# The last wo's fourth rows by four transfers of eight partitions, and the unread products ahead of the last values

## The chip, the cores and the metric

The kernel runs on one core of a Trainium2 chip. The metric is the device time of one execution in microseconds; the median of the runs is compared. A profiled execution of the same program gives the views that are quoted.

## The reference

A decode step for 8 sequences: a grouped-query attention over a cache of 8192 positions and, on the same normalised input, a dense layer with Mish and a second dense layer. Both results and the input are added up.

```python
xn = _layernorm(x)                                   # x: 8 x 1 x 512
q = (xn @ wq).reshape(B, Sq, 32, 128)                # 32 heads, 8 of keys and values
scores = einsum("bhqd,bhkd->bhqk", q, k) * 128**-0.5 # k, v: 8 x 8 x 8192 x 128
o = einsum("bhqk,bhkd->bhqd", softmax(scores), v)
a = o.reshape(B, Sq, 4096) @ wo                      # wo: 4096 x 512
h = xn @ w1 + b1                                     # w1: 512 x 1792
m = (h * tanh(softplus(h))) @ w2                     # w2: 1792 x 512
return x + a + m
```

All is float32. The caches are 537 MB of the 561 MB that are read.

## The kernel before

The work goes in 16 packs (`PACKS`) of two batch entries (`PB`) and two key heads; four pairs of key heads (`PAIRS`) with four packs each. For each pack and batch entry (b = 0, 1) one block of keys and one block of values is loaded, 8 MB each. `scores` multiplies the keys, `rows`, `maximum`, `exponents`, `fold` and `weights` make the softmax weights on ACT and DVE, `values` multiplies the weights with the values of the pack before, `gather` and `merge` turn the result into columns `oT`. After four packs `turn` transposes the pair's `oT` into `oW`, and `outputs` multiplies it with the pair's part of `wo`. One TensorE instruction of float32 shows as two matmul records and two weight loads.

All loads are issued by the SP queue, in the order of a list (`queue`). There are three places in SBUF: `kva`, `kvb` (20 rows of 1024 numbers on each partition) and `kvw` (four rows). A load is taken from the head of the list (`pump`) once its place is free by the program's order, and the DMA instruction then waits for those matmuls that still read the columns that it overwrites. The DMA completions are told by eight semaphores, handed out in turn.

At the end the list holds the values of the last pack, for b = 0 into `kvb` and for b = 1 into `kva` in two parts (three quarters and one), and then six pieces: `w2` in four parts (`W2_PARTS`: two, two, two and one of seven rows), into `kvb`, and between them the last pair's `wo` in two halves, into `kvw`. Each partition's part of a pair's `wo` is four rows of 1024 numbers (`OR = 4`); a half is two rows of all 128 partitions.

The program's last steps, in the order in which PE gets them:

```python
values(0, landed["v", p, 0]); gather(p, 0); sums(p, lsel.pop(p)); merge(p, 0); add_up()
values(1, landed["v", p, 1], 0, ROUNDS * 3 // 4)
values(1, landed["v", p, 1], ROUNDS * 3 // 4); gather(p, 1)
down(*W2_PARTS[0], w2_sb)
keep_busy(2)
merge(p, 1); turn(PAIRS - 1, tid)
down(*W2_PARTS[1], w2_sb); last_outputs(0, OR // 2, wo_sb)
down(*W2_PARTS[2], w2_sb); last_outputs(OR // 2, OR, wo_sb)
down(*W2_PARTS[3], w2_sb)
```

`down` (L628) multiplies the Mish result with parts of `w2`, 16 matmuls for two rows of it; `last_outputs` (L562) the last pair's `oW` with rows of `wo`, 8 matmuls for a row: two heads, four groups of 128 output columns. Both add into the same PSUM tile `H`, as `add_up` (L548) does, which starts it. `turn` (L514) writes `oW` from PSUM by four copies of 32 partitions each, two on DVE (L528) and two on ACT (L526), which follow one upon the other. `keep_busy(n)` (L639) makes n matmuls of 512 columns into a PSUM tile that nobody reads afterwards; they only keep TensorE at work. After the last `down` DVE copies `H` (L718) and SP stores it (L719).

Of the kernel before, what the change touches and what calls it, by code (L numbers as in the profile page):

```python
# [8 lines left out]
F32 = mybir.dt.float32  # L9
# [4 lines left out]
P = 128  # L14
B = 8
# [8 lines left out]
G = 4  # L24
# [3 lines left out]
BW = 1024  # L28
# [4 lines left out]
Q = P // G  # L33
# [5 lines left out]
PAIRS = HKV // 2  # L39
NP = B // PB  # L40
PACKS = PAIRS * NP
R = P // G
# [22 lines left out]
QR = CC  # L65
OR = 4
W1R = 2 * CC * P // P
W2R = G * FT // 2 * FP // P
FAR = 1e38

# [2 lines left out]
def kernel(  # L73
# [12 lines left out]
    nc = tc.nc  # L86
# [3 lines left out]
    work = ctx.enter_context(tc.tile_pool(name="work", bufs=2))  # L90
# [4 lines left out]
    place = {n: const.tile([P, size], F32, name=f"kv{n}") for n, size in sizes.items()}  # L95
    queue = []
    taken, landed = {}, {}

    def rows_of(blocks):

        return blocks.rearrange("j p f -> (j p f)").rearrange("(p f) -> p f", p=P)
# [12 lines left out]
    def plan(what, at, blocks, parts=((0, 1),), lo=0):  # L114

        rows = rows_of(blocks)
        n = rows.shape[1]
        t = place[at][:, lo : lo + n]

        def load(cols):  # L120
            nc.sync.dma_start(t[:, cols], rows[:, cols])
            return t

        for first, end in parts:
            cols = slice(round(first * n), round(end * n))
            queue.append((what, at, lambda cols=cols: load(cols)))


    sc = const.tile([P, 512], F32, name="sc")
# [7 lines left out]
    def blocks_of(src, p, b):  # L137
        i, k = divmod(p, NP)
        lo = ((k * PB + b) * HKV + 2 * i) * NB
        return src[lo : lo + KN]  # L140
# [3 lines left out]
    def plan_k(p, b):  # L144
        if (p, b) == (0, 1):
            plan(("k", p, b), "a", blocks_of(kT, p, b))
        else:
            up[0] = KX * BW - up[0]
            plan(("k", p, b), "b", blocks_of(kT, p, b), lo=up[0])

    def plan_v(p, b, at, parts=((0, 1),)):
        plan(("v", p, b), at, blocks_of(v, p, b), parts)

# [3 lines left out]
    def plan_wo(i, parts=((0, 1),)):  # L157
        plan(("wo", i), "w", wo[i * 4 : i * 4 + 4], parts)
# [8 lines left out]
    for p in range(PACKS):  # L167
        for b in range(PB):
            plan_k(p, b)
            if (p, b) in between:  # L170
                what, i = between[p, b]
                (plan_wq if what == "wq" else plan_wo)(i)
            if p > 0:
                plan_v(p - 1, b, "a")
    plan_v(PACKS - 1, 0, "b")
    plan_v(PACKS - 1, 1, "a", ((0, 3 / 4), (3 / 4, 1)))
    W2_PARTS = ((0, 2), (2, 4), (4, 6), (6, 7))
    for k, (lo, hi) in enumerate(W2_PARTS):
        plan("w2", "b", w2, ((lo / W2R, hi / W2R),))
        if 0 < k < 3:  # L180
            plan_wo(PAIRS - 1, (((k - 1) / 2, k / 2),))


    S = psum.tile([P, GK], F32, name="s")
# [34 lines left out]
    xnT = const.tile([P, QR, 2, Q], F32, name="xnT")  # L219
    aT = const.tile([P, 2 * W2R, Q], F32, name="aT")  # L220
    xw = aT.rearrange("p j q -> p (j q)")[:, : W1R * 2 * B]
    xw = xw.rearrange("p (r t b) -> p r t b", r=W1R, t=2)

    def setup():
# [33 lines left out]

        wide = scratch[:B, 2 * D : 2 * D + W1R * P]
        for t in range(2):  # L260
            nc.gpsimd.tensor_copy(
                wide.rearrange("b (r c t i) -> b r c t i", r=W1R, c=CC, t=2)[:, :, :, t, :],
                xc.rearrange("b (c i r) -> b r c i", c=CC, r=W1R),
            )
# [26 lines left out]
    def setup_w1(wide):  # L291
        for r in range(W1R):
            nc.tensor.transpose(
                M[:, 64 + r * B : 64 + (r + 1) * B], wide[:, r * P : (r + 1) * P], ident[:B, :B]
            )
        for t in range(2):
            nc.vector.tensor_scalar(
                xw[:, :, t, :],
                M[:, 64 : 64 + W1R * B].rearrange("p (r b) -> p r b", r=W1R),
                half[:, t : t + 1],  # L300
                None,
                op0=ALU.mult,
            )

        nc.gpsimd.memset(pt, 0.0)
# [148 lines left out]
    def values(b, vt, lo=0, hi=ROUNDS):  # L454


        for k in range(lo, hi):
            for c in range(G):
                j = G * k + c
                nc.tensor.matmul(  # L460
                    O[b][Q * c : Q * (c + 1), :],
                    pt[:, b, j % 2, j // 2].rearrange("p t e h -> p (t e h)"),
                    vt[:, W4 * DH * j : W4 * DH * (j + 1)],
                    start=(k == 0),
                    stop=(k == ROUNDS - 1),
                )

    def gather(p, b):

        os = OS[p, b] = work.tile([P, DH], F32, name="os")  # L470
        nc.vector.tensor_scalar(os, O[b][:, :DH], isel[:, 0:1], None, op0=ALU.mult)  # L471
        for i in range(1, W4):
            nc.vector.scalar_tensor_tensor(  # L473
                os,
                O[b][:, DH * i : DH * (i + 1)],
                isel[:, i : i + 1],
                os,
                op0=ALU.mult,
                op1=ALU.add,
            )  # L480

    oT, oW = {}, {}

    def merge(p, b):

        i, k = divmod(p, NP)
        at = 168 + b * 2 * REP
        nc.tensor.matmul(M[:, at : at + 2 * REP], OS.pop((p, b)), hsel, start=True, stop=True)  # L488
        if b == PB - 1:
            if k == 0:  # L490
                oT[i] = work.tile([P, 2, REP, B], F32, name="oT")
            nc.vector.tensor_mul(  # L492
                oT[i][:, :, :, k * PB : (k + 1) * PB].rearrange("p e h b -> p (e h) b"),
                M[:, 168 : 168 + PB * 2 * REP].rearrange("p (b r) -> p r b", b=PB),
                RT.pop(p).rearrange("p b e h -> p (e h) b"),
            )
# [10 lines left out]
    def turn(i, tid):  # L507


        to = oW[i] = work.tile([P, OR, 2, B], F32, name="oW")  # L510
        o = oT.pop(i).rearrange("p n h b -> p (n h b)")
        cols = 2 * REP * B
        for r in range(OR):
            nc.tensor.matmul(  # L514
                M[:, 256 + r * cols : 256 + (r + 1) * cols],
                tid[:, r].rearrange("p g i -> p (g i)"),
                o,
                start=True,
                stop=True,
            )  # L520
        m = M[:, 256 : 256 + OR * cols].rearrange("p (r j q) -> p j r q", r=OR, j=G)
        for j in range(G):
            rows = slice(Q * j, Q * (j + 1))
            dst = to[rows].rearrange("p r h b -> p r (h b)")
            if i == PAIRS - 1 and j % 2:
                nc.scalar.copy(dst, m[rows, j])  # L526
            else:
                nc.vector.tensor_copy(dst, m[rows, j])  # L528

    def outputs(i, w):  # L530

# [13 lines left out]
    def add_up():  # L545

        for g in range(G):
            nc.tensor.matmul(  # L548
                H[Q * g : Q * g + B, :P],
                rsel[:, :B],  # L550
                acc[:, g * P : (g + 1) * P],
                start=True,
                stop=False,
            )

    def last_outputs(lo, hi, w):

        for r in range(lo, hi):
            for h in range(2):
                for g in range(G):  # L560
                    at = r * BW + h * D + g * P
                    nc.tensor.matmul(  # L562
                        H[Q * g : Q * g + B, :P],
                        oW[PAIRS - 1][:, r, h, :],
                        w[:, at : at + P],
                        start=False,
                        stop=False,
                    )

    def mish(w1_sb):  # L570
# [42 lines left out]
        for e in range(2):  # L613
            nc.vector.tensor_mul(
                act.rearrange("p (i a e l) -> p e a l i", a=2, e=2, i=W2R)[:, e],
                h[:, half * e : half * (e + 1)].rearrange("p (a l i) -> p a l i", a=2, i=W2R),
                t1[:, half * e : half * (e + 1)].rearrange("p (a l i) -> p a l i", a=2, i=W2R),
            )
# [4 lines left out]
    def down(lo, hi, w):  # L623

        for j in range(2 * lo, 2 * hi):
            for g in range(G):
# [5 lines left out]
                    start=False,  # L632
                    stop=(j == 2 * W2R - 1),
                )

    def keep_busy(n):

        for k in range(n):
            nc.tensor.matmul(C[0][:Q, :], ones[:, :Q], acc, start=True, stop=True)  # L639
# [19 lines left out]
    for p in range(PACKS):  # L659
        for b in range(PB):  # L660
            k = landed.pop(("k", p, b))

            n = PB * p + b - (p > 0)
# [15 lines left out]
            if (p, b) in between:  # L679
                what, i = between[p, b]  # L680
# [14 lines left out]
    p = PACKS - 1  # L695
# [5 lines left out]
    sums(p, lsel.pop(p))  # L701
    merge(p, 0)
    add_up()
    values(1, landed["v", p, 1], 0, ROUNDS * 3 // 4)
    values(1, landed["v", p, 1], ROUNDS * 3 // 4)
    gather(p, 1)
    w2_sb, wo_sb = landed["w2"], landed["wo", PAIRS - 1]
    down(*W2_PARTS[0], w2_sb)
    keep_busy(2)
    merge(p, 1)  # L710
    turn(PAIRS - 1, tid)
    down(*W2_PARTS[1], w2_sb)
    last_outputs(0, OR // 2, wo_sb)
    down(*W2_PARTS[2], w2_sb)
    last_outputs(OR // 2, OR, wo_sb)
    down(*W2_PARTS[3], w2_sb)
    res = acc[:, :P]
    nc.vector.tensor_copy(res, H[:, :P])  # L718
# [3 lines left out]
    last = {}  # L722
# [54 lines left out]
```

## Time and profile before

| | |
|---|---|
| median of 3 runs | 1311.3 us (1311.26 to 1312.05) |
| profiled execution | 1311.37 us, of which its span 1309.6 us |
| busy in the span | PE 879.2 us (67%), PEld 282.3 us (22%), DVE 385.2 us (29%), ACT 111.6 us (9%) |
| mean granted TensorE clock | 0.823 |
| DMA | 561.76 MB in 11590 packets, 429 GB/s |

Busy times of the engines overlap each other. PE is TensorE's matmul, PEld its weight load, SPq the queue of SP that issues the loads. In the windows, "DMA share" is the mean busy share of the core's 16 DMA engines, counted by the packets that start in the window; over short windows it can pass 1. In the timeline and the chain the first number is the start in us from the span's start, the second the duration, xN the number of records merged into the line.

### The profile page before, as it was taken

The numbers are of one execution on the slowest core, as the hardware profiler recorded it, in microseconds if no ns is written. First come the engines' busy times: TensorE is split into PE (matmuls) and PEld (weight loads), VectorE is DVE, ScalarE is ACT, GpSimd is POOL, SyncE is SP. The second block draws the span as 40 slices with busy tenths as digits, with TensorE's granted clock in tenths as the row PEclk, the third lists the DMA queues.
The fourth block names the chain that finished last, engine by engine and source line by source line (L and its number), as shares of the span: only waits on it lengthen the run. The fifth ranks groups of instructions, "written<-read, shape, count | busy, mean of one in ns | idle before, by whom it ended". The sixth has DMA issues, their size and how long they took to land.

```text
span 1309.6 us, 10699 instructions
## 1 busy us (share of the span) xinstructions
PE 879.2 (67%) x4768; PEld 282.3 (22%) x4768; DVE 385.2 (29%) x590; ACT 111.6 (9%) x294; POOL 4.8 (0%) x10
## 2 busy tenths in 40 slices
PE   4886667866567766677666686665775666766567
PEld 1221112212112221122211222121221221222113
DVE  7150504205050230522305033052320505114051
ACT  1020101001010100101101010010100101001010
POOL 1000000000000000000000000000000000000000
PEclk9887788887789877797777887778887779878778
DMA  9999999999999999999999999999999999999997
GB/s 406 440 427 437 437 427 428 440 433 431 432 435 429 433 437 425 443 421 445 419 442 421 418 448 425 441 421 443 423 437 432 429 433 421 443 427 435 437 425 333
DMA packets 11590, 561.76 MB, mean 429 GB/s; under 512 B 1292, under 2 KB 1424, under 8 KB 1560
## 3 DMA queue, kind: packets, MB, share of 16 engines
q1 hardware_dynamic: 11520, 561.06, 99.3%
q8 instruction: 37, 0.61, 0.2%
q14 instruction: 9, 0.07, 0.0%
q10 hardware_dynamic: 24, 0.02, 0.0%
HBM read 561.01 MB, written 0.07 MB: 428 GB/s over the span
## 4 chain that ended last, share of the span: by engine, by line
DMA 61%; PE 35%; DVE 3%; issue 0%; ACT 0%; SPq 0%; DVEq 0%; ACTq 0%
DMA kvb<-in_kT 52%; PE c L353 30%; PE o L460 3%; DMA kva<-in_v 3%; DMA kva<-in_kT 3%; DMA kvb<-in_w 2%; DMA kvb<-in_v 2%; DVE raw L412 1%; DVE pt L430 1%; PE h L312 0%; PE o L581 0%; PE s L365 0%; DVE raw L421 0%; DVE nm L379 0%; DVE os L473 0%
## 5 line engine op out<-in xcount | busy, mean ns | idle before, releaser
L353 PE MATMUL c<-kvb,qT 128*64 128x512 f32 x1984 | 500.7, 669 | 334.4 <-DMA kvb<-in_kT 302.3
L353 PEld LDWEIGHTS c<-kvb,qT 128*64 128x64 f32 x1984 | 161.7, 154 | 673.3 <-issue 424.4
L460 PE MATMUL o<-kva,pt 128*32 128x512 f32 x1984 | 251.4, 665 | 26.2 <-DMA kva<-in_v 26.2
L379 DVE TENSOR_REDUCE nm<-s 128x1 f32<-128x1024 f32 x16 | 19.6, 1225 | 454.7 <-PE s L365 454.7
L412 DVE STREAM_TRANSPOSE raw<-e 128x2048 f32<-128x2048 f32 x32 | 116.2, 3630 | 14.3 <-ACT e L404 12.7
L460 PEld LDWEIGHTS o<-kva,pt 128*32 128x32 f32 x1984 | 67.1, 121 | 200.3 <-issue 161.1
L360 ACT COPY sc<-c 128x512 f32<-128x512 f32 x32 | 18.7, 585 | 1003.4 <-PE c L353 1003.4
L404 ACT ACTIVATE e<-s,nms 128x512 f32<-128x512 f32 x128 | 86.2, 685 | 126.3 <-DVE nms L393 66.8
L492 DVE TENSOR_TENSOR oT<-m,r 128x16 f32<-128x16 f32 x16 | 2.8, 174 | 234.1 <-PE m L488 234.1
L471 DVE TENSOR_SCALAR os<-o,isel 128x128 f32<-128x128 f32 x32 | 11.2, 351 | 160.1 <-PE o L460 160.1
L430 DVE TENSOR_TENSOR pt<-raw 64x256 f32<-64x256 f32 x128 | 53.6, 419 | 2.0
L365 PE MATMUL s<-sc,csel 64*128 64x512 f32 x128 | 38.0, 672 | 8.4 <-ACT sc L360 8.4
L421 DVE TENSOR_TENSOR raw<-raw 128x1024 f32<-128x1024 f32 x32 | 39.2, 1226 | 1.1
L340 DVE TENSOR_TENSOR qT<-qc,bsel 128x1024 f32<-128x1024 f32 x32 | 37.7, 1219 | 0.0
L473 DVE SCALAR_TENSOR_TENSOR os<-o,isel,os 128x128 f32<-128x128 f32 x96 | 33.7, 351 | 3.4
L404 ACT ACTIVATION_READ_ACCUMULATOR e<-s,nms 128x1 f32 x128 | 26.0, 203 | 0.0
L380 PE MATMUL m<-ident,nm 128*1 128x128 f32 x16 | 4.3, 270 | 21.2 <-DVE nm L379 21.2
L312 PE MATMUL h<-kvw,xnT 128*64 128x512 f32 x64 | 17.6, 699 | 0.0
L488 PEld LDWEIGHTS m<-hsel,os 128*128 128x128 f32 x64 | 9.5, 188 | 28.5 <-issue 24.4
L323 DVE TENSOR_SCALAR e<-h 128x512 f32<-128x512 f32 x16 | 9.9, 684 | 17.2 <-PE h L312 17.2
L488 PE MATMUL m<-hsel,os 128*128 128x8 f32 x64 | 12.4, 266 | 3.1 <-DVE os L473 1.6
L353 PE MATMUL c<-kva,qT 128*64 128x512 f32 x64 | 14.0, 593 | 0.6 <-DMA kva<-in_kT 0.6
(100 smaller groups left out, 164.6 us busy)
## 6 DMA issues: line engine op xcount, KB each, us to landing
kvw<-in_wq SPq DMA_DIRECT2D x4, 2048.0 KB, 30.4
kvw<-in_wo SPq DMA_DIRECT2D x3, 2048.0 KB, 29.6
kva<-in_v SPq DMA_DIRECT2D x1, 6144.0 KB, 26.1
kva<-in_w SPq DMA_DIRECT2D x1, 3584.0 KB, 15.7
kvb<-in_w SPq DMA_DIRECT2D x3, 1024.0 KB, 21.0
kva<-in_v SPq DMA_DIRECT2D x1, 2048.0 KB
kvw<-in_wo SPq DMA_DIRECT2D x2, 1024.0 KB, 24.8
kvb<-in_w SPq DMA_DIRECT2D x1, 512.0 KB
```

The lines of the kernel that those rows point to most:

```text
L340: nc.vector.tensor_mul(qT[:, b], qc[:, k * PB + b] .rearrange("p r (o h) -> p r o h", o=1) .to_broadcast([P, KR, KN, REP]), bsel.rearrange ...
L353: nc.tensor.matmul(C[b][HE * c : HE * (c + 1), :], t[:, r], k[:, r * BW + c * 512 : r * BW + (c + 1) * 512], start=(r == order[0]), stop=( ...
L360: nc.scalar.copy(sc, C[b])
L365: nc.tensor.matmul(S[:, c * 512 : (c + 1) * 512], csel[HE * c : HE * (c + 1), b].rearrange("p u b h -> p (u b h)"), sc[HE * c : HE * (c + ...
L379: nc.vector.tensor_reduce(nm, S, axis=AX.X, op=ALU.max, negate=True)
L404: nc.scalar.activation(ex[:, :, s, :], S[:, c * 512 : (c + 1) * 512].rearrange("p (t f) -> p t f", t=HT), AF.Exp, bias=NMS[p][:, s : s + 1 ...
L412: nc.vector.transpose(raw.rearrange("p (m t r) -> p t m r", m=TW, t=HT), ex.rearrange("p t s (q m) -> p t m (s q)", m=TW),)
L421: nc.vector.tensor_add(raw[:, :, :n], raw[:, :, :n], raw[:, :, n:])
L430: nc.vector.tensor_add(pt[rows, b, c].rearrange("p m t e h -> p (m t) e h")[:, :, e], raw[rows, :, at : at + REP], raw[rows, :, V8 + at : ...
L460: nc.tensor.matmul(O[b][Q * c : Q * (c + 1), :], pt[:, b, j % 2, j // 2].rearrange("p t e h -> p (t e h)"), vt[:, W4 * DH * j : W4 * DH * ...
L473: nc.vector.scalar_tensor_tensor(os, O[b][:, DH * i : DH * (i + 1)], isel[:, i : i + 1], os, op0=ALU.mult, op1=ALU.add,)
L488: nc.tensor.matmul(M[:, at : at + 2 * REP], OS.pop((p, b)), hsel, start=True, stop=True)
```

## The change

The last pair's `wo` no longer comes as two halves. Its first two rows of all partitions come as one load of 1 MB, its third row as one of 512 KB, both into `kvw` as before. The fourth rows of all partitions, 512 KB, come to partitions 0 to 31 of `kvb`, behind the seven rows of `w2`: partition q gets four rows, the fourth rows of partitions q, q + 32, q + 64 and q + 96. Four transfers bring them, each to eight partitions (every fourth one of the 32), in runs of 4 KB. They stand ahead of `w2`'s first part in the list, so that ten transfers follow the values where there were six: the four, then `w2` in four parts with the two loads of `wo` between them.

`turn` writes, for the last pair, into the tile `sc`: the first three rows to all partitions as before, and by a fifth copy, on DVE, the fourth rows' four groups to partitions 0 to 31. `last_outputs` then takes the four groups (`OM` to `OX`, 32 matmuls over 32 partitions) right after `w2`'s second part, then rows one and two, and after `w2`'s third part row three. `keep_busy` makes four matmuls instead of two, and stands ahead of the values of b = 1 instead of behind `w2`'s first part.

```diff
+OM = OR - 1
+OX = OM + G
...
+    def plan_last(what, at, blocks, n, size, lo):
+
+        rows = rows_of(blocks).rearrange("(g e k) (r f) -> k r e g f", g=G, k=R // 8, r=n)
+        t = place[at][:, lo : lo + G * size].rearrange("p (g f) -> p g f", g=G)
+
+        def load():
+            for k in range(R // 8):
+                nc.sync.dma_start(t[k : R : R // 8], rows[k, n - 1])
+            return place[at]
+
+        queue.append((what, at, load))
...
+    WO_PARTS = ((0, 2), (2, 3))
+    WO_AT = W2R * BW
+    plan_last("w2", "b", wo[(PAIRS - 1) * 4 :], OR, BW, WO_AT)
     for k, (lo, hi) in enumerate(W2_PARTS):
         plan("w2", "b", w2, ((lo / W2R, hi / W2R),))
         if 0 < k < 3:
-            plan_wo(PAIRS - 1, (((k - 1) / 2, k / 2),))
+            lo, hi = WO_PARTS[k - 1]
+            plan_wo(PAIRS - 1, ((lo / OR, hi / OR),))
...
-        to = oW[i] = work.tile([P, OR, 2, B], F32, name="oW")
+        if i < PAIRS - 1:
+            to = work.tile([P, OR, 2, B], F32, name="oW")
+        else:
+            to = sc[:, : OX * 2 * B].rearrange("p (r h b) -> p r h b", r=OX, h=2)
+        oW[i] = to
...
+        last = i == PAIRS - 1
         for j in range(G):
             rows = slice(Q * j, Q * (j + 1))
-            dst = to[rows].rearrange("p r h b -> p r (h b)")
-            if i == PAIRS - 1 and j % 2:
-                nc.scalar.copy(dst, m[rows, j])
+            n = OM if last else OR
+            dst = to[rows, :n].rearrange("p r h b -> p r (h b)")
+            if last and j % 2:
+                nc.scalar.copy(dst, m[rows, j, :n])
             else:
-                nc.vector.tensor_copy(dst, m[rows, j])
+                nc.vector.tensor_copy(dst, m[rows, j, :n])
+        if last:
+            dst = to[:Q, OM:].rearrange("p j h b -> p j (h b)")
+            nc.vector.tensor_copy(dst, m[:Q, :, OM])
...
         for r in range(lo, hi):
+            n = P if r < OM else Q
...
-                        oW[PAIRS - 1][:, r, h, :],
-                        w[:, at : at + P],
+                        oW[PAIRS - 1][:n, r, h, :],
+                        w[:n, at : at + P],
...
     add_up()
+    keep_busy(4)
     values(1, landed["v", p, 1], 0, ROUNDS * 3 // 4)
     values(1, landed["v", p, 1], ROUNDS * 3 // 4)
     gather(p, 1)
-    w2_sb, wo_sb = landed["w2"], landed["wo", PAIRS - 1]
+    w2_sb, wo_sb = place["b"], place["w"]
     down(*W2_PARTS[0], w2_sb)
-    keep_busy(2)
     merge(p, 1)
     turn(PAIRS - 1, tid)
     down(*W2_PARTS[1], w2_sb)
-    last_outputs(0, OR // 2, wo_sb)
+    last_outputs(OM, OX, w2_sb[:, WO_AT - OM * BW :])
+    last_outputs(*WO_PARTS[0], wo_sb)
     down(*W2_PARTS[2], w2_sb)
-    last_outputs(OR // 2, OR, wo_sb)
+    last_outputs(*WO_PARTS[1], wo_sb)
     down(*W2_PARTS[3], w2_sb)
```

## The prediction

> **What bounds the kernel now.** I read the page first, then the chain of work that ended last, then the windows over the last 30 us, then the timeline of the same stretch.
>
> ```profile
> span 1309.6 us, 10699 instructions
> DMA  9999999999999999999999999999999999999997
> q1 hardware_dynamic: 11520, 561.06, 99.3%
> q8 instruction: 37, 0.61, 0.2%
> q10 hardware_dynamic: 24, 0.02, 0.0%
> HBM read 561.01 MB, written 0.07 MB: 428 GB/s over the span
> ```
>
> The kernel is a stream of 561 MB. The DMA engines are busy in nines in every slice but the last, so the change, which moves the same bytes and touches nothing before the last two packs' end, can only work in that last slice.
>
> ```profile
> 1278.87 27.12 DMA kvb<-in_w
> 1305.99 0.04 issue
> 1306.03 0.67 PE h L628 x16
> 1306.70 0.02 issue
> 1306.72 0.29 DVE acc L718
> ```
>
> The chain's end: the last load of w2 is issued at 1278.87, lands at 1305.99, and then only 16 matmul records, one copy and the store follow. The end of the kernel is that landing plus a fixed 0.98 us of work and the store. So the first question is what sets the landing.
>
> ```profile
> core 0: us, PE busy (x) PEld busy (x) DVE busy (x) ACT busy (x) POOL busy (x), PEclk, DMA share, GB/s
> 1280.00:1285.00 5.00, 2.43 (x28) 0.89 (x20) 1.57 (x5) 0.00 (x0) 0.00 (x0) 1.00 0.84 360
> 1285.00:1290.00 5.00, 2.46 (x12) 0.59 (x16) 0.00 (x0) 0.00 (x0) 0.00 (x0) 0.60 0.98 415
> 1290.00:1292.00 2.00, 2.00 (x16) 0.59 (x12) 0.00 (x0) 0.00 (x0) 0.00 (x0) 0.50 0.99 414
> 1292.00:1294.00 2.00, 2.00 (x20) 0.44 (x13) 0.00 (x0) 0.00 (x0) 0.00 (x0) 0.79 1.02 426
> 1296.00:1298.00 2.00, 2.00 (x45) 1.12 (x38) 0.68 (x2) 0.00 (x0) 0.00 (x0) 1.00 1.01 422
> 1301.00:1302.00 1.00, 1.00 (x29) 0.93 (x32) 0.21 (x1) 0.20 (x1) 0.00 (x0) 1.00 0.82 336
> 1302.00:1303.00 1.00, 0.96 (x40) 0.67 (x32) 0.22 (x1) 0.20 (x1) 0.00 (x0) 1.00 0.62 258
> 1303.00:1304.00 1.00, 1.00 (x48) 1.00 (x40) 0.00 (x0) 0.00 (x0) 0.00 (x0) 1.00 0.44 172
> 1304.00:1305.00 1.00, 0.65 (x26) 0.36 (x20) 0.00 (x0) 0.00 (x0) 0.00 (x0) 1.00 0.26 107
> 1305.00:1306.00 1.00, 0.86 (x32) 0.57 (x24) 0.00 (x0) 0.00 (x0) 0.00 (x0) 1.00 0.06 25
> ```
>
> The DMA share is the point here. It does not stop, it fades: 0.82, 0.62, 0.44, 0.26, 0.06. Times 16 engines that is 13, 10, 7, 4 and 1 at work: every engine has had its equal part of every load, but they are staggered, and the last load has landed only when the last engine is done. Added up, 2.20 us of full work is left at 1301.0; shared evenly it would be over at 1303.2, where the packets really go on to about 1305.6. So 2.4 us is all that any evening out can bring, 0.18% of the run. One engine moves 422 GB/s over 16, 26.4 GB/s (row 1296 to 1298): 64 KB take it 2.48 us, 32 KB 1.24 us.
>
> ```profile
> 1261.37 2.04 SPq L121 DMA_DIRECT2D kva<-in_v  x2
> 1272.93 8.45 PE L460 MATMUL o<-kvb,pt 128*32 128x512 f32 x64 [7.88 <-DMA kvb<-in_v]
> 1274.92 1.70 SPq L121 DMA_DIRECT2D kvb<-in_w  x2
> 1277.92 0.43 SPq L121 DMA_DIRECT2D kvb<-in_w  x1
> 1283.49 0.41 PE L548 MATMUL h<-acc,rsel 128*8 128x128 f32 x8
> 1287.54 9.67 PE L460 MATMUL o<-kva,pt 128*32 128x512 f32 x64 [3.64 <-DMA kva<-in_v]
> 1297.04 1.05 PE L628 MATMUL h<-kvb,aT 128*8 128x128 f32 x32
> 1297.67 1.12 DVE L473 SCALAR_TENSOR_TENSOR os<-o,isel,os 128x128 f32<-128x128 f32 x3
> 1297.91 1.88 PE L639 MATMUL c<-acc,ones 128*32 128x512 f32 x4
> 1299.72 0.39 PE L488 MATMUL m<-hsel,os 128*128 128x8 f32 x2
> 1300.38 1.10 PE L514 MATMUL m<-oT,e 128*128 128x64 f32 x8 [0.27 <-DVE oT L492]
> 1302.00 0.22 DVE L528 COPY oW<-m 32x64 f32<-32x64 f32 x1 [0.27 <-ACT oW L526]
> 1302.26 0.20 ACT L526 COPY oW<-m 32x64 f32<-32x64 f32 x1 [0.29 <-DVE oW L528]
> 1302.52 1.06 PE L562 MATMUL h<-kvw,oW 128*8 128x128 f32 x32
> 1303.39 1.06 PE L628 MATMUL h<-kvb,aT 128*8 128x128 f32 x32
> 1304.80 1.06 PE L562 MATMUL h<-kvw,oW 128*8 128x128 f32 x32 [0.35 <-DMA kvw<-in_wo]
> ```
>
> The timeline shows that PE is nearly as late as the transfers: from 1287.54 it runs almost without a hole, and waits for a load only at 1304.80 (0.35 us) and at 1306.03. The second half of wo lands at 1304.76 or so and the last half megabyte of w2 at 1305.99, 1.23 us later, which is the pace of 32 KB to an engine. Counted back at 2.48 us a megabyte, w2's third part landed near 1302.3, wo's first half 1299.8, w2's second part 1297.3, its first 1294.9, and the last quarter of v 1292.4 (estimates from the two landings and the pace).
>
> **The fourth rows on eight engines.** Before, wo's second half is one megabyte over all 16 engines, 64 KB each; now its fourth rows, 512 KB, come by four transfers of eight partitions. What an eight-partition transfer does is seen at the start: the loads of x (8 rows) and of b1 (4 rows) are all of queue q10, and left 24 packets, which is one data packet and one completion for each of 8 and 4 engines. So the four transfers should run on the same eight engines, 64 KB each (4 x 4 rows x 4 KB), where every engine had 32 KB. Eight engines get 1.24 us more, eight get 1.24 us less; the end depends on which. [...]
>
> [...] No view names an engine. But the packets of one engine join end to start, and followed so from the beginning the instruction packets (q8) fall on about half of the engines; the four that carried b1 are none of these, nor are most of those that carried x. An engine that also carries 16 KB instruction packets is late by that much. So I take it that the eight without the fourth rows are the late ones. The late ones then land 1305.99 - 1.24 = 1304.75. The eighth engine in order of finishing is done where the share passes one half, about 1303.3, and the landing is told 0.4 us after the packets (1305.99 against 1305.6): 1303.7, plus 1.24 is 1304.9. The last landing is the later of the two, 1304.9, a gain of 1.1 us. Bounds: 2.4 us gained if the two groups even out entirely, 1.24 us lost if a late engine is among the eight.
>
> Small packets: rows of 4 KB are what w2's last part has, and its 32 KB took 1.23 us, the full pace. I take no extra price; half the pace for all 64 KB would be the other end, +2.48 us on eight engines.
>
> **The order of the queue.** The fourth rows stand ahead of w2 in SP's queue and go to columns 7168 to 11263 of kvb, which the values of the first batch read until their 22nd of 32 matmuls: 1272.93 + 22/32 x 8.45 = 1278.7 instead of 1274.92 for the first load of w2. Four issues at 0.43 us (row 1277.92) put w2's first part at 1280.5. In front of it in the engines are the 8 MB of v issued from 1261.37 on, which last until 1292.4 on the slowest engine, so 10 us of cover, and no cost. Then a new wait: the completion semaphores are eight, handed out in turn, and in the changed program as built the first half of wo waits for the landing of v's three quarters (1287.5), w2's third part for that of v's last quarter (1292.4), and the last two for the first two of the four transfers. What is queued behind on SP is only the rest of these loads, and PE waits for them. At 1292.4 the earliest engine is some 4.5 us ahead (the fade from 1301 to 1305.6), but has the fourth rows, two parts of w2 and wo's first two rows in front of it, 9.9 us; 5.4 us of cover stay against an issue of 0.43 us. No cost; without the cover the last parts would come that much later.
>
> **PE.** The unread products go from two (1.88 us between w2's first part and the merge) to four, ahead of the values. PE is idle there from 1283.90 to 1287.54, and the clock falls: 1.00, then 0.60, 0.50, 0.79. Four of them take twice 1.88 at most, 3.8 us, against a hole of 3.64: 0.1 us late at worst. If they hold the clock at 1.00, the values, which now take 9.67 us, take the sum of granted clock over that stretch (the row of 0.60 is one microsecond at 1.00 and four at 0.50): 2.46 x 0.5 + 2 x 0.5 + 2 x 0.79 + 3.21 = 7.0 us. They end at 1294.6 instead of 1297.2. The sum from there: gather 1.58 us (1297.21 to 1298.79 before), so the merge starts at 1296.2, where before it waited for the products until 1299.72. From merge to the last copy were 2.74 us (1299.72 to 1302.46); one copy more at the copies' pitch of 0.26 makes 3.0: 1299.2. The fourth rows now need 32 matmuls where 8 did, 2.12 us by the row of 16 in 1.06: until 1301.3. Rows one and two 1.06 until 1302.4; w2's third part, landed by then, until 1303.5; row three, half of 1.06, needs a landing near 1303.7 and is done at 1304.2. Then PE waits for the last landing at 1304.9, with 0.7 us to spare. The matmuls on 32 partitions are not in the trace; 66 ns each as on 128 is my value, nothing saved and nothing lost, since they stream the same 128 columns.
>
> **The sum.** The profiled execution took 1311.37 us for a span of 1309.6; 1311.37 - 1.1 = 1310.3. The median before is 1311.3, 0.07 under the profiled one, so the same to a tenth: 1310.3 us.
>
> **Rivals.**
> *A late engine is among the eight.* Then it gets 1.24 us more: last landing 1307.2, 1312.5 us. It decides as soon as one of the four engines still at work after 1304 carries the fourth rows. Against it is the way the instruction packets fall; for it, that two of x's engines could not be told from the late ones. Chance 0.14.
> *The products do not hold the clock.* Then the values still end at 1297.2, the merge starts at 1298.8, and by the same steps PE ends row three at 1306.6 and the last part at 1307.2, 0.5 us behind the 1306.70 of now: the transfers' gain is hidden behind PE, 1311.8 us. [...] Against: the hole that lowers the clock is filled whole. Chance 0.10.
> *The clock falls later.* The products no longer stand between w2's first part and the merge, and PE has small holes at 1296 and 1299. Two half-speed stretches of 3.4 us there would cost 3.4 us of PE work less 0.7 spare: 1313 us or a little above. Chance 0.08.
> *The change does more than this*, the two groups even out and other engines' stagger shrinks: up to 2.4 us, 1308.9 us. Chance 0.08.
> *The eight-engine transfers run at half pace*: 1303.7 + 1.24 + 2.48 = 1307.4, 1312.8 us. Chance 0.04. [...]
> The forecast keeps 0.56.
>
> **The numbers.** The likeliest case gives 1310.3. Below it the range goes to 1309.4, part of the way to full evening; above to 1312.6, which takes in the late engine and the lost clock and leaves out the fallen clock and the half pace. 0.2%, 2.6 us, is about what a measurement of this kernel can tell from no change, and of all cases only the fullest evening comes near it from below (0.07 that it is passed, with the spread of runs) and the fallen clock or half pace from above (0.11). Same: 0.82.
>
> **What would show it.** Right: the DMA share stays near 1 longer and then falls in a steeper fade, over by 1304.6; the last load of w2 lands at about 1304.9; the clock is 1.00 through the values, which take 7 us; PE waits before the last two groups. Wrong: a share that ends in a long tail of few engines after 1305 (a late engine got the rows), a PE that reaches the last part after its landing, or issues of w2 that land after the engines ran dry.

## The result, and the profile after

The changed kernel takes 1314.11 us (median of 21 runs, 1311.05 to 1316.99), the kernel before 1311.46 us (21 runs, 1311.25 to 1313.49) on the same chips. The ratio is 1.0021 (95% interval 1.0015 to 1.0027): 2.65 us slower, where 1.1 us faster was forecast. The changed kernel's runs also spread over 6 us, those of before over 2. Its profiled execution took 1313.89 us, 0.2 us under the median.

From the page, then from the chain of work that ended last:

```profile
span 1312.1 us, 10810 instructions
DMA  9999999999999999999999999999999999999997
```

```profile
1280.56 0.86 SPq L161
...
1283.62 14.42 DMA kvb<-in_w
1298.08 1.90 PE h L659 x32
1299.97 0.54 PE m L507 x2
1300.77 1.97 PE m L539 x8
1302.73 1.83 PE h L659 x32
1304.56 2.91 PE h L593 x96
1307.47 0.87 PE h L659 x32
1308.35 0.44 PE h L593 x16
1308.78 0.48 PE h L659 x16
```

Before, the chain was one landing at 1305.99 and 0.67 us of PE. Now it enters PE much earlier: the *first* part of w2 lands at 1298.03, and from there PE's own work is the chain for 11 us, to the end. The windows show why that work takes so long (columns as in the prediction's windows):

```profile
1285.00:1290.00 5.00, 5.00 (x31) 1.54 (x33) 0.00 (x0) 0.00 (x0) 0.00 (x0) 1.00 0.97 409
1290.00:1292.00 2.00, 2.00 (x24) 0.73 (x20) 0.00 (x0) 0.00 (x0) 0.00 (x0) 1.00 0.98 375
...
1296.00:1298.00 2.00, 0.00 (x0) 0.00 (x0) 0.60 (x2) 0.00 (x0) 0.00 (x0) 0.96 1.02 426
1298.00:1301.00 3.00, 2.65 (x35) 1.80 (x36) 0.17 (x1) 0.00 (x0) 0.00 (x0) 0.50 0.99 412
...
1302.00:1303.00 1.00, 1.00 (x12) 0.82 (x15) 0.20 (x1) 0.00 (x0) 0.00 (x0) 0.50 0.78 320
1303.00:1304.00 1.00, 1.00 (x28) 0.72 (x20) 0.42 (x2) 0.38 (x2) 0.00 (x0) 0.50 0.49 201
1304.00:1305.00 1.00, 1.00 (x28) 0.48 (x24) 0.00 (x0) 0.00 (x0) 0.00 (x0) 0.66 0.17 70
1305.00:1306.00 1.00, 1.00 (x48) 0.87 (x40) 0.00 (x0) 0.00 (x0) 0.00 (x0) 1.00 0.16 57
1306.00:1307.00 1.00, 1.00 (x44) 0.76 (x36) 0.00 (x0) 0.00 (x0) 0.00 (x0) 1.00 0.07 29
1307.00:1308.00 1.00, 1.00 (x48) 0.99 (x40) 0.00 (x0) 0.00 (x0) 0.00 (x0) 1.00 0.02 8
```

Two things are to be seen. The DMA share does fall more steeply up to 1304 (0.49 to 0.17 in a second), as forecast, but then has the long tail that the prediction named as the sign of a late engine: 0.16, 0.07 and 0.02 are 2.6, 1 and 0.3 of 16 engines. And the clock, held at 1.00 through the values, is 0.50 from about 1297.8 to 1304.7 (0.96 over two microseconds is 0.16 us at half; 0.66 over one is 0.68). The timeline has the hole ahead of that:

```profile
1284.58 3.17 PE L670 MATMUL c<-acc,ones 128*32 128x512 f32 x7
...
1287.96 7.08 PE L479 MATMUL o<-kva,pt 128*32 128x512 f32 x61
1298.08 1.90 PE L659 MATMUL h<-kvb,aT 128*8 128x128 f32 x32 [3.04 <-DMA kvb<-in_w]
...
1304.49 1.99 PE L593 MATMUL h<-kvb,sc 32*8 32x128 f32 x64
```

The products filled the hole ahead of the values, the values took 7.08 us, as forecast, and ended at 1295.0 (1294.6 was forecast). Then PE stands idle for 3.04 us for w2's first part. The hole was not removed, but moved behind the values, where all that follows is the tail.

### The profile page after: what moved, and what is told of

Its sections match the earlier page's. It is cut to its first block, busy times and chain, and to the rows that moved or that the text cites. A ratio compares the mean times of both kernels' runs of the same rounds, so it can differ in the third digit from the quotient of the medians.

```text
span 1312.1 us, 10810 instructions
## 1 busy us (share of the span) xinstructions
PE 866.5 (66%) x4820; PEld 282.5 (22%) x4820; DVE 384.2 (29%) x591; ACT 111.5 (9%) x294; POOL 4.8 (0%) x10
## 4 chain that ended last, share of the span: by engine, by line
DMA 63%; PE 34%; DVE 2%; issue 0%; SPq 0%; ACT 0%; ACTq 0%; DVEq 0%
DMA kvb<-in_kT 56%; PE c L372 31%; DMA kva<-in_kT 3%; DMA kvb<-in_v 2%; PE o L479 2%; DMA kva<-in_w 1%; DMA kvb<-in_w 1%; DVE raw L431 1%; DVE pt L449 0%; PE o L612 0%; PE h L659 0%; DVE nm L398 0%; PE s L384 0%; PE h L593 0%; SPq L161 0%
## 5 line engine op out<-in xcount | busy, mean ns | idle before, releaser
L479 PE MATMUL o<-kva,pt 128*32 128x512 f32 x1984 | 233.3, 624 | 24.2 <-DMA kva<-in_v 24.2
```

What stands on the lines that cost most here:

```text
L479: nc.tensor.matmul(O[b][Q * c : Q * (c + 1), :], pt[:, b, j % 2, j // 2].rearrange("p t e h -> p (t e h)"), vt[:, W4 * DH * j : W4 * DH * ...
```

## The experiments

Theory A: the tail on PE sets the end (a hole, half clock, 24 more matmuls). Theory B: the last landing sets it (a late engine among the eight). Each ratio is to the kernel before, run on the same chip.

**The change in halves.** First the products alone, on the kernel before:

```diff
     add_up()
+    keep_busy(4)
     values(1, landed["v", p, 1], 0, ROUNDS * 3 // 4)
...
     down(*W2_PARTS[0], w2_sb)
-    keep_busy(2)
```

> The kernel before with one part of the change alone: four unread products ahead of the last values instead of two behind w2's first part; all loads as before. Theory A (the loss comes from the fourth rows on eight engines: two engines that also carry instruction packets are among the eight, their part of the last load lands late, w2's first part too, and PE then stands idle and loses its clock): the last load lands at 1306.0 as before, the values take 7 us, PE waits for the landings, 1311.4 us, the same as before within 0.5. Theory B (the loss comes from PE: the products no longer bridge the hole behind the values, the clock falls): the clock is 0.50 somewhere between 1295 and 1305 and the time is 1313 to 1314.5 us.

1311.53 us, 1.0002 (0.9993 to 1.0011): no difference. Its timeline:

```profile
1285.32 4.87 PE L639 MATMUL c<-acc,ones 128*32 128x512 f32 x7
...
1290.05 7.00 PE L460 MATMUL o<-kva,pt 128*32 128x512 f32 x60
...
1306.19 0.62 PE L628 MATMUL h<-kvb,aT 128*8 128x128 f32 x16 [0.18 <-DMA kvb<-in_w]
```

Here the clock fell beside the products (0.66 over 1285 to 1290); they took 4.9 us instead of 3.2, and the values began some 2 us after their load had landed. The end still is the landing.

Then all of the new PE program with the old loads, and the new loads with the old PE program. Both cuts are against the changed kernel; in the second `turn` and its tile are also those of before again:

```diff
-    plan_last("w2", "b", wo[(PAIRS - 1) * 4 :], OR, BW, WO_AT)
...
-            lo, hi = WO_PARTS[k - 1]
-            plan_wo(PAIRS - 1, ((lo / OR, hi / OR),))
+            plan_wo(PAIRS - 1, (((k - 1) / 2, k / 2),))
```

> The loads of the kernel before (wo in two halves, no small transfers) under the changed program of PE, DVE and ACT: the 32 matmuls on 32 partitions read columns of kvb that hold old values, so the last pair's fourth rows are left out of the result. Theory A (the loads on eight engines make the loss): the last load lands at 1306.0, the clock holds, PE is ready for it or half a microsecond late, 1311.4 to 1312.0 us. Theory B (PE's longer program makes it): 1313 us or more, with PE past the last landing.

```diff
-    keep_busy(4)
     values(1, landed["v", p, 1], 0, ROUNDS * 3 // 4)
...
     down(*W2_PARTS[0], w2_sb)
+    keep_busy(2)
...
-    last_outputs(OM, OX, w2_sb[:, WO_AT - OM * BW :])
-    last_outputs(*WO_PARTS[0], wo_sb)
+    last_outputs(0, OR // 2, wo_sb)
     down(*W2_PARTS[2], w2_sb)
-    last_outputs(*WO_PARTS[1], wo_sb)
+    last_outputs(OR // 2, OR, wo_sb)
```

> The loads of the changed kernel under the program of the kernel before: the fourth rows land in kvb and are not read, and the matmuls of the fourth row read what an earlier wo left in kvw, so the fourth rows are left out of the result. Theory A: the last load lands between 1305.7 and 1308.5 as in the three profiles with these loads, PE waits for it, 1312.5 to 1313.5 us. Theory B: 1311.4 us within 0.4, the program of before being back.

The program alone takes 1311.54 us, 1.0000 (0.9991 to 1.0009); the loads alone 1312.17 us, 1.0002 (0.9994 to 1.0011). Their last groups on the timeline, first the program alone, then the loads alone:

```profile
1306.40 0.62 PE L657 MATMUL h<-kvb,aT 128*8 128x128 f32 x16
```

```profile
1306.88 0.62 PE L644 MATMUL h<-kvb,aT 128*8 128x128 f32 x16 [0.19 <-DMA kvb<-in_w]
```

Neither half has the loss (the loads alone may have a part of it: 0.7 us by the medians, inside the interval). The program alone has no wait named at its last group: PE is level with the landing, with nothing to spare. The loads alone land late (1306.88), but PE has room. Together the late loads meet a PE without slack.

**How the fourth rows come.** One transfer to 32 partitions instead of four of eight; four of eight neighbouring partitions; four of 16 partitions (every fourth of 64, two rows to each), the last also with the products as two and two. The cut shows the transfers alone; the order of `rows` goes with them, and for the 64 partitions two copies and 16 matmuls over 64 partitions instead of one and 32:

```diff
-            for k in range(R // 8):
-                nc.sync.dma_start(t[k : R : R // 8], rows[k, n - 1])
+            nc.sync.dma_start(t[:R], rows[n - 1])                    # one of 32
+                nc.sync.dma_start(t[8 * k : 8 * (k + 1)], rows[k, n - 1])  # neighbours
+                nc.sync.dma_start(t[k : 2 * R : 4], rows[k, n - 1])  # every fourth of 64
```

> The changed kernel, but the fourth rows come by one transfer of 32 partitions instead of four of eight, so that all 16 engines can share it; PE's program is the changed one. Theory A: every engine has 32 KB of it as before the change, w2's first part lands at about 1295.5 instead of 1298.0, the last load at 1306.0 to 1306.5, the clock stays at 1.00, 1311.4 us within 0.7. Theory B: nothing changes for PE, 1313 to 1315 us. A third theory (runs of 4 KB into 32 partitions are slow on whatever engines): the last load still lands a microsecond late, 1312.5 us.

> The changed kernel with each of the four transfers going to eight partitions in a row (0 to 7, 8 to 15, ...) instead of every fourth one; same bytes, same runs of 4 KB, same number of engines. If the slow single transfer of 32 partitions (1318.8 us) was slow because several engines then write into the same few partitions, these are slow too: four or eight engines on neighbouring partitions at a time, the GB/s of the windows from 1288 to 1298 fall well under 400, 1316 us or more. If it was slow for the rows that it reads (one run of 4 KB in 16), or for 32 partitions as a whole, this is no slower than the changed kernel: 1313 to 1315 us.

> The changed kernel, but the fourth rows come to 64 partitions, two to each, by four transfers of 16 partitions (every fourth one), so that all 16 engines get 32 KB each as before the change; two copies bring them into place instead of one, and 16 matmuls over 64 partitions multiply them instead of 32 over 32. Theory late engine, the loss in the landing comes from the two late engines among the eight: the last landing goes back to 1306.0, as before the change, from the 1307.2 that is the mean of eight profiles with the four transfers of eight; the time falls by 1.2 us at least, and by up to 1.1 us more for the 16 matmuls where the clock is down in the tail: 1311.4 to 1312.4 us. Theory crowding, any transfer in runs of 4 KB to every fourth partition slows all: the landing stays at 1307 or later, 1313 us or more.

> The kernel of the 64 partitions, with the unread products as two ahead of the last values and two behind them. Theory late engine: landing 1306.0 and a PE that waits for it, 1311.4 us, level with the kernel before and at least 1 us under the same products with eight-partition transfers (1312.65 us). A version that beats the kernel before would need a landing below 1306.0, which nothing here gives. Theory crowding: 1312.6 us or more.

1318.80 us (1.0054, 1.0042 to 1.0067); 1318.24 (1.0054, 1.0039 to 1.0069); 1314.69 (1.0023, 1.0014 to 1.0032); and 1314.69 (1.0024, 1.0014 to 1.0034). One window of the first three, in this order:

```profile
1292.00:1294.00 2.00, 2.00 (x26) 0.56 (x17) 0.00 (x0) 0.00 (x0) 0.00 (x0) 1.00 0.97 215
```

```profile
1292.00:1294.00 2.00, 2.00 (x24) 0.68 (x23) 0.00 (x0) 0.00 (x0) 0.00 (x0) 1.00 0.96 199
```

```profile
1292.00:1294.00 2.00, 1.13 (x12) 0.13 (x4) 0.00 (x0) 0.00 (x0) 0.00 (x0) 1.00 1.07 279
```

The engines are busy all the time, yet move 199 to 279 GB/s where the changed kernel's own row has 414 (375 in the one before it). Packets of other loads take longer too while such a transfer passes: the values' packets of 16 KB took 0.99, 1.11 and 0.85 us (medians of 1288.5 to 1296) where the changed kernel has 0.61. The 4-KB runs are the same in all of them, so it isn't the runs; what differs is which partitions each transfer writes. The run on 64 partitions was slowed as well (279 GB/s), so it could not tell what it was made for. Why these ways are slow and that of the changed kernel is not, no run shows.

**Where PE's tail stands.** Four kernels move or drop the products (the number in each place):

| | ahead of the last values | behind them, ahead of w2's first part | behind w2's first part |
|---|---|---|---|
| changed kernel | 4 | 0 | 0 |
| products twice | 4 | 4 | 0 |
| products back | 0 | 0 | 2 |
| two and two | 2 | 2 | 0 |
| none | 0 | 0 | 0 |

One more, one group, drops three quarters of the new matmuls:

```diff
-    last_outputs(OM, OX, w2_sb[:, WO_AT - OM * BW :])
+    last_outputs(OM, OM + 1, w2_sb[:, WO_AT - OM * BW :])
```

> The changed kernel with four more unread products between the values and w2's first part, to bridge the hole of 3.0 us in PE. Theory A: the last load still lands at about 1308, the clock holds, and the time is the landing plus what was there before, 1313.3 us, with less spread than the changed kernel's 1311.05 to 1316.99. Theory B: the loss is gone, 1311.4 us or less.

> The changed kernel with the unread products as before the change: two, behind w2's first part. Theory A: the last load lands as late as in the changed kernel (about 1308), the values run at half clock and end at 1297, so that PE is hardly idle ahead of w2's first part; 1313 to 1314 us, no better than the landing allows. Theory B: back to the time before, 1311.4 us within 0.5, if PE's longer program does not take the half microsecond that it is behind.

> Only the first of the fourth rows' four groups is multiplied, 8 matmuls instead of 32; the other three groups are left out of the result, their transfers and all else stay. Theory A, PE's tail at half clock sets the end: 24 matmuls less, 48 records of 33 to 66 ns, are 1.6 us at full and up to 3 us at half clock, so the loss of 2.65 us against the kernel before shrinks to about 1 us or less, 1312.4 us. Theory B, the last landing sets the end (1307.9 in the changed kernel's profile, with 0.4 us of PE work lying between it and the last group): 0.5 us at most is gained, 1313.6 us.

> Two of the four unread products stand ahead of the last values, the other two behind them, ahead of w2's first part, in the hole of 3 us that PE has there. Theory A, the hole lowers the clock for the tail and PE's tail then sets the end: the clock stays at 1.00 from the end of the values on, PE is done with row three about 1306, and the time is that of the kernel before or up to 1 us above it, 1311.5 to 1312.5 us. Theory B, the last landing: the clock may hold, but the time stays at 1313.5 to 1314 us.

> The unread products are left out altogether. If they hold no clock and only stand in the way of the values (in four of the profiles the clock fell beside them and they took 4.9 us), the time is that of the changed kernel or below, 1312 to 1314 us. If they did hold it and that matters, the values take 9.7 us, end at 1297.2, and the first part of w2 follows almost without a hole; the clock may then fall at 1298 all the same for lack of work before, and the time is 1314 to 1315 us.

| | us | ratio (95%) |
|---|---|---|
| products twice | 1313.94 | 1.0016 (1.0007 to 1.0025) |
| products back | 1313.33 | 1.0011 (1.0002 to 1.0019) |
| one group | 1312.90 | 1.0009 (1.0000 to 1.0017) |
| two and two | 1312.65 | 1.0011 (1.0002 to 1.0020) |
| none | 1312.44 | 1.0008 (0.9999 to 1.0017) |

The last group of twice, and of back:

```profile
1308.46 0.62 PE L659 MATMUL h<-kvb,aT 128*8 128x128 f32 x16
```

```profile
1308.53 0.62 PE L659 MATMUL h<-kvb,aT 128*8 128x128 f32 x16
```

Twice holds the clock from 1288.5 to the end, but its eight products cost PE about as much time as the clock gives back; the last landing was at 1305.74 here, so PE alone set the end. In back the last landing itself was 1308.49. Two and two has the tail as the prediction wanted it; a window and the last group:

```profile
1304.00:1305.00 1.00, 0.84 (x32) 0.55 (x26) 0.00 (x0) 0.00 (x0) 0.00 (x0) 1.00 0.22 78
```

```profile
1307.10 0.62 PE L659 MATMUL h<-kvb,aT 128*8 128x128 f32 x16 [1.68 <-DMA kvb<-in_w]
```

At a full clock PE has 1.68 us to spare before the last landing, and the time is still 1.3 us above the kernel before, which took 1311.37 us on that chip. With no products at all:

```profile
1287.66 8.77 PE L479 MATMUL o<-kva,pt 128*32 128x512 f32 x64 [2.71 <-DMA kva<-in_v]
...
1307.16 0.62 PE L659 MATMUL h<-kvb,aT 128*8 128x128 f32 x16 [0.61 <-DMA kvb<-in_w]
```

the values are slower, the hole behind them is only 0.82 us, the clock stays up afterwards (1.00 from 1292 on), and the landing binds again. So theory A holds for part of the loss: 1314.11 against 1312.65 and 1312.44 is 1.5 to 1.7 us by the medians, and one group, with 24 matmuls less, gave 1.2 us of it back (the intervals of these ratios overlap that of the changed kernel, so the split is good to about 1 us). What remains, 1.1 to 1.3 us, is theory B's.

**The landing by dose.** On the two-and-two kernel, two of the four transfers, and none:

```diff
-            for k in range(R // 8):
+            for k in range(R // 16):                                     # two
-    plan_last("w2", "b", wo[(PAIRS - 1) * 4 :], OR, BW, WO_AT)           # none
```

> The kernel with two unread products ahead of the last values and two behind them (1312.65 us, last landing 1307.05 in its profile), but only the first two of the four transfers of fourth rows are issued: 16 of the 32 partitions keep old numbers, and their part of the result is left out. The eight engines get 32 KB each, as much as each engine had before the change, the other eight 1.24 us less. Theory late engine, one or two of the eight also carry instruction fetches and finish last: the last landing is that of before, 1306.0, and the time 1311.4 us. Theory of the prediction, the late ones are among the other eight: landing 1304.9, 1310.2 us.

> The same kernel with none of the four transfers; the fourth rows' part of the result is left out, their 32 matmuls run on old numbers. Every engine has 1.24 us less to carry than before the change. Theory late engine: last landing 1306.0 - 1.24 = 1304.8, PE about level with it, 1310.2 us, so that the three kernels with 0, 2 and 4 transfers stand 1.2 us apart each. Theory of the prediction: 1304.8 and 1310.2 us too, no different from two transfers.

Four, two and no transfers: 1312.65, 1311.72 (1.0003, 0.9994 to 1.0012) and 1310.32 us (0.9993, 0.9984 to 1.0002). The last groups of two and of none:

```profile
1305.30 0.62 PE L659 MATMUL h<-kvb,aT 128*8 128x128 f32 x16 [0.52 <-DMA kvb<-in_w]
```

```profile
1304.81 0.62 PE L658 MATMUL h<-kvb,aT 128*8 128x128 f32 x16 [0.50 <-DMA kvb<-in_w]
```

The medians stand 0.9 and 1.4 us apart (those of the spans 1.1 and 1.2), 2.33 in all, where 64 KB of one engine take 2.48. Were the late ones among the other eight, two and none would be the same, so the times speak for a last engine among the eight; but neighbouring doses' intervals overlap, and those of four and none only touch at 1.0002. The landings of the single profiles (1307.05, 1305.26, 1304.77) go the same way with unequal steps. In the profile of two the last engine is one *without* fourth rows, which had finished the values last of all, at 1292.87; the last of the eight landed at 1304.94. (How an engine is told is said below.) That profile's span, 1308.9 us, is 0.8 under the median span of its runs, so it is not typical, and what the step from none to two is made of stays open.

**The transfers behind w2's first part.** To take away the hole behind the values, the four transfers go behind that part in the queue, and their matmuls ahead of w2's second part:

```diff
-    plan_last("w2", "b", wo[(PAIRS - 1) * 4 :], OR, BW, WO_AT)
     for k, (lo, hi) in enumerate(W2_PARTS):
         plan("w2", "b", w2, ((lo / W2R, hi / W2R),))
+        if k == 0:
+            plan_last("w2", "b", wo[(PAIRS - 1) * 4 :], OR, BW, WO_AT)
```

> The changed kernel with the four transfers behind w2's first part instead of ahead of it, and their matmuls ahead of w2's second part. Theory A with its second step (w2's first part lands late behind the fourth rows, PE stands idle and its clock halves): w2's first part lands at 1295, PE has no hole of 3 us there, the last landing is as late as in the changed kernel, 1312.5 to 1313 us, 1 to 1.5 less than the changed kernel. If the hole does not matter: 1314 us as the changed kernel.

1315.08 us, 1.0021 (1.0012 to 1.0030), no better:

```profile
1299.62 2.99 PE L594 MATMUL h<-kvb,sc 32*8 32x128 f32 x64 [1.22 <-DVE sc L559]
```

The first hole shrank to 0.39 us, but with nothing of w2 left to lie beside the five copies, PE waits 1.22 us for the last of them; the clock falls at 1300 (0.58 over 1300 to 1302, then 0.50 up to 1307) and the tail is late again (its last group began at 1307.83, the last landing was 1307.79). No version tried beats the kernel before with the whole work done.

## Why the prediction was wrong

**Even out by eight engines: the step that failed.** "The eighth engine in order of finishing is done where the share passes one half, about 1303.3 ...: 1303.7, plus 1.24 is 1304.9" took the eight engines with the fourth rows for the first eight to finish, and put nothing on them but the 1.24 us. The trace has a record for each engine's completion of each load, 16 for one to all partitions. With four, two and none of the transfers 176, 160 and 144 packets under 512 B start behind 1279, so eight engines complete each transfer. No view prints them by engine, but a load of 1 MB is done on each engine some 2.48 us after the one before it (before, the last at 1292.38, 1294.86 and 1297.33), so the times of successive loads can be joined.

In the changed kernel the engines finished the last quarter of the last values between 1288.35 and 1292.38. From there one without fourth rows took 12.37 us to the end of its part of the last load (1292.38 to 1304.75), so one with them should take 14.85. The eight were six of the first seven, and the ninth and tenth, done at 1290.18 and 1290.34. At full pace these two would have landed at 1305.0 and 1305.2; they landed at 1306.09 and 1307.94. Their fourth rows took 3.54 and 3.63 us instead of 2.48. And on the last engine w2's first part took 4.06 us instead of 2.48: a 16-KB packet of instructions came in between (0.89 us from 1293.94 on), and the 8-KB packet behind it took 0.86 us instead of 0.31. The sum 1290.34 + 14.85 + 1.15 + 1.58 = 1307.92 is the measured landing.

The sentence "So I take it that the eight without the fourth rows are the late ones" held as far as it goes: the six engines that finished the values last were all without them, and the last of these landed at 1304.75, the figure forecast. It did not follow that the other eight would be done by 1304.9.

The eight profiles with these four transfers landed last at 1307.94, 1305.74, 1308.49, 1306.83, 1307.79, 1306.75, 1307.05 and 1307.11 (changed kernel, twice, back, loads alone, behind w2's first part, one group, two and two, none), each time on one of the eight; the mean is 1307.2. In the seven with the transfers ahead of w2, the last of the eight to finish the values was done at 1290.34 to 1292.00, where a landing at 1304.9 needs about 1290.0. In at least four (changed kernel, back, loads alone, two and two) an instruction packet cost one of the eight 1.5 to 1.6 us. The argument had used these packets only to say which engines are late already.

**Rows of 4 KB at full pace** held in four of those seven profiles (2.5 us of fourth rows on the last of the eight), not in the changed kernel (3.6), back (3.0) and none (2.7). In the changed kernel the row of 1290 to 1292 shows it: 375 GB/s at a share of 0.98. What slows them in some runs stays open.

**PE: the same error a second time.** "The sum from there: gather 1.58 us ..., so the merge starts at 1296.2" left out that w2's first part stands ahead of the merge on PE, and that its load now comes behind the fourth rows. Had the eight been the first eight, it would have landed at about 1295.1 and cost nothing (1303.7 is 2.3 us ahead of 1305.99; 1294.9 less 2.3, plus 2.48). It landed at 1298.03. A delay that was weighed for the end of the queue was not carried to the loads in between. From this came the 3.04-us hole, the fallen clock and a tail of 11.1 us (1298.08 to 1309.22) that takes 9.2 us at a full clock (the kernel without products, 1297.25 to 1307.78 less 1.33 us of waits).

**The products.** "If they hold the clock at 1.00" held in this profile, 7.08 us against 7.0 forecast. In the profiles of products alone, of products twice, of the program alone, of one transfer of 32 and of neighbours the clock fell all the same, and they took 4.9 us, where "0.1 us late at worst" was said. In the traces the granted clock keeps a value for 3.41 us or a multiple of it (in the changed kernel 0.50 for 6.83 us behind the hole, two such steps). Counted on from the last change, a step begins at 1283.0 to 1284.2 in the four profiles where four products ahead of the values held the clock, and at 1285.0 to 1285.8 in the five where it fell. So it seems to hang on where the steps lie; no run varies that, so it is not shown.

**The rivals.** Two came true together: the late engine (1312.5 us, and 1312.65 was measured where the clock held) and "The clock falls later". Each had been priced with the other absent: the first counted PE as on time, the second gave the landing 0.7 us of slack. The late landing is what opened the hole, so they were not independent. That the first rival's landing, 1307.2, is the mean of the eight profiles is partly luck: its condition, that an engine which is late already carries fourth rows, held in two of the seven profiles (in loads alone and none, one of the three that finished the values last is of the eight), and elsewhere engines from the middle were made late.

**What held.** No cost of the queue's order was seen: w2's first part was issued at 1283.62 instead of 1280.5, but the rows shown keep a DMA share of 0.97 to 1.02 up to 1301. Nor did the extra copy and the 24 matmuls cost anything on a PE that starts on time: the program alone stands at 1.0000. That 32 partitions save nothing was right: 1.93 us at full clock for 32 matmuls in the profiles at a full clock, 2.12 forecast.

## What to carry to other kernels

When a load is moved from 16 engines to eight, look for the one engine that finishes last: in all eight profiles with the four transfers the last landing, 1305.74 to 1308.49, was on one of the eight, and an argument about the group did not find it. Place each of the eight in the order of finishing (the completion records of successive loads can be joined), add what small rows and instruction packets may cost one engine (here up to 1.15 and 1.6 us), and put the delay on every load behind it in the queue, not only on the last. The hole on PE that was filled in one place (3.64 us ahead of the values) opened where the next load was late (3.04 us behind them), and near the end it also halved the clock for 6.83 us of what follows. Price such rivals together if one causes the other.

## What was unexpected of the hardware

The fourth rows' 512 KB pulled all of the stream down from some 415 to 199 to 279 GB/s (1292 to 1294) while they passed, at a DMA share of 0.96 to 1.07, when they came by one transfer to 32 partitions, by four transfers with eight neighbouring partitions each, or by four to every fourth of 64 partitions; by the changed kernel's four to every fourth of 32, with eight engines to each, they left 375 to 414 (the changed kernel from 1290 to 1294). The DMA share alone doesn't show this, only the share beside the GB/s. One 16-KB packet of instructions cost the engine that carried it 1.5 to 1.6 us where it could be followed; 16 KB of the values take 0.61. And in five of the nine profiles with four products ahead of the values, TensorE's clock fell at about 1285 beside them (0.66 over 1285 to 1290), though they left no hole.
